# Re-ordering the prologue of a fused attention and GEGLU block: loads, statistics, transposes and weight re-ordering

## The chip, the cores and the metric

The kernel runs on one core of a Trainium2 chip. The metric is the time of one execution in microseconds (us) of device time. The engines named below are PE (TensorE, matmuls), DVE (VectorE), ACT (ScalarE), POOL (GpSimd) and SP (SyncE, which here only issues DMAs). Each engine executes its own list of instructions in order; they wait for each other with semaphores.

## The reference

One sequence of S = 2048 tokens of width D = 512, 32 heads of 16, and a GEGLU of width F = 1792, all bf16:

```python
def reference(A_x, A_wqkv, A_wo, B_x, B_w_gate, B_w_up, B_w_down):
    # _A_ref: q, k, v = split(x @ wqkv); p = softmax(q k^T / 4); (p v) @ wo
    # _B_ref: (gelu(x @ w_gate) * (x @ w_up)) @ w_down
    x = A_x
    h = x + _A_ref(_layernorm(x, axis=-1), A_wqkv, A_wo)
    h2 = h + _B_ref(_layernorm(h, axis=-1), B_w_gate, B_w_up, B_w_down)
    return h2
```

(`...` bodies are told in the comments; `_layernorm` has no weights, gelu is the tanh form.)

## The kernel before, in words

**How it is recorded.** `Plan` (line 16) records one instruction list per engine; `P.op` and `P.dma` add an instruction with the tiles that it reads and writes, and `Plan` derives the semaphore waits. So the order on each engine is the order in which the Python code calls `P.op`, fixed when the program is built.

**Tiles.** The 2048 tokens are 16 tiles `t` of 128, or 4 chunks `c` of 512. A *unit* is one *group* `gi` (256 queries, 8 groups) and one *slot* (4 heads, 8 slots): 64 units. For a unit, pass 1 computes the scores of all keys (line 772) and reduces their maximum on DVE (line 781, one reduce of 128x1024 a tick); POOL turns the maxima into a correction that is added to the queries (lines 792 to 826); pass 2, 24 ticks later, computes the scores again (line 842), ACT takes the exponential from PSUM to `PTM`, `PTE` or `PTG` (line 854), and PE multiplies by V (line 868, `item_pv`). A unit has 16 *ticks*; the main loop (line 1259) runs 1024 ticks of pass 1 and 24 more of pass 2 alone, 1048 in all. In the first 20 ticks (`DOUBLES`) the scores of two ticks are issued together.

**The dense stream.** All other PE work goes through `Dense` (line 482), a queue of items that the loop feeds piece by piece into the ticks: projections `item_projT` (K and Q, head tile `ht`, chunk `c`, line 645) and `item_projV` (line 709), transposes `item_xnT` (line 461), and after them, per group, `item_ofin`, `item_oproj`, and the FFN: seven pairs of `item_gate` and `item_up` (lines 1052 and 1066) and two `item_down` (line 1103). The list `qkv_items` (line 731) sets the order at the start. When its last item is done, `qkv_finished` (line 626) frees the SBUF of the projections and queues the FFN weights in twelve pieces, of which one is loaded in four of every 16 ticks (line 1312); the first group's FFN may start when all are issued (`add_ffn_when`, line 937). Items start under conditions that the builder estimates (bank free, ACT's lag `act_lag`, POOL's budget in `PoolStream`). A piece that does not fill its share of a tick is made up with dummy matmuls (line 1252).

**GELU by hand.** For groups 0 to 6 the gate tile is evicted to `g_sb`, three POOL operations (lines 1037 to 1039) prepare the argument, ACT takes the tanh (line 1030), two POOL operations (1035, 1036) and the product with `u_sb` (1089) write two chunks of `GUT`, which `item_down` reads. For the last group (7), ACT takes the GELU directly from PSUM (line 1060).

**The end.** `tail_b` (line 1196) closes the last unit's attention (`tail_norm`, `tail_onT`), the output projection, the second layer norm of group 7 (two POOL operations for the reciprocal root, lines 1217 and 1218; normalisation on DVE, line 1220), and in between feeds what is left in the dense stream (`fill`, line 1145). Then come the rest of the dense stream (line 1226), and the FFN of group 7 (line 1232).

**The prologue**, which the change touches. SP issues four loads of x (one a chunk), the Q and K weights as one load of 1024 KB, the V weights, and `wo`. Layer norm of a tile needs its statistics: by `stats_dve` (bn_stats and bn_aggr on DVE, line 355) or `stats_act` (two ACT passes with accumulation, line 359), then the reciprocal root on POOL (`rstd_bn`, `rstd_sums`, `rstd_pow`), then the normalisation (`norm1`, on DVE or POOL; `c3_act` on ACT). The normalised tile is transposed either by `xnT_pe` (four PE transposes, evicted by ACT, line 391) or by `xnT_dma` (a DMA transpose issued by SP, line 399; chunk 2 only). `w_order` (line 402) copies the Q or K weights of a head tile to the order in which the projection reads them. `warm` (line 413) issues dummy matmuls. The first two items, K and Q of the first head tile and chunk, are evicted directly to `KT` and `QT` (lines 661 and 659). `early` (line 754) says at which tick the rest of the prologue is issued: statistics and normalisation of chunk 3, and `w_order` for head tiles 1 to 3.

```python
        warm(16)
        for t in range(4):
            stats_dve(t)
        ...
        for t in range(4, 7):
            stats_act(t)
        stats_dve(7)
        stats_dve(8)
        ...
        for t in range(4):
            norm1(t, "dve")
            xnT_pe(t, 4 + t)
        warm(3)
        stats_dve(9)
        w_order("k", 0, "dve")
        w_order("q", 0, "dve")
```

## Time and profile before

| | |
|---|---|
| median of 3 runs | 1260.45 us (1260.25 to 1260.73) |
| the profiled execution | 1260.49 us, span 1258.8 us, mean granted PE clock 0.997 |
| busy of the span | PE 90%, DVE 95%, ACT 95%, POOL 60% |
| first reduce of line 781 starts | 16.97 us |
| thirteenth reduce starts | 36.48 us |
| last exponential of line 854 starts in the row at | 1225.38 us |
| weights for Q and K landed | 12.04 us after the span's start (issued 2.94, 9.1 to landing) |
| longest groups | DVE line 781, 1024 reduces, 1166.1 us; ACT line 854 to `PTM`, 1388 exponentials, 741.0 us |

All times within the profile are counted from the start of the span, of one profiled execution. A row of the timeline has its start, its duration, the engine, the line, the operation, `out<-in` with shapes, how many instructions are merged, and in brackets how long the engine idled before it and who ended the wait. "PEld" is the loading of weights into PE.

### The profile page before, as it was taken

The page shows a single profiled execution, that of the slowest core. Times are in us where ns is not written, and L with a number is a line of the kernel's source. Part 1 is how long each engine was busy: PE and PEld are TensorE (multiplying, and loading weights), DVE is VectorE, ACT ScalarE, POOL GpSimd, SP SyncE. Part 2 cuts the span into 40 slices and gives each one's busy share as a digit, 9 for nine tenths or more (in the row PEclk, how much of TensorE's full clock was granted, in tenths as well). Part 3 has the DMA queues.
Part 4 walks back from the last instruction along what each step waited for, and adds up shares of the span by engine and source line. Part 5 has one row for each costly group of instructions (what it writes and reads, how often), then busy time and mean ns, then how long its engine had stood idle before and what let it go on. Part 6 is the DMA issues. An engine that isn't in the chain of part 4 may idle for free.

```text
span 1258.8 us, 31261 instructions
## 1 busy us (share of the span) xinstructions
PE 1133.1 (90%) x12501; PEld 405.6 (32%) x12680; DVE 1194.0 (95%) x1090; ACT 1200.2 (95%) x2465; POOL 759.3 (60%) x1534
## 2 busy tenths in 40 slices
PE   6999888889999999989989998999999899899998
PEld 2322222233323333333323333233333333233335
DVE  8999999999999999999999999999999999999913
ACT  7799999999999999999999999999999999999992
POOL 7557775467746765386745766467653766457650
PEclk9999999999999999999999999999999999999999
DMA  5000004300010000100010000100001000100000
GB/s 166 27 26 27 24 18 123 93 5 4 6 30 12 6 5 6 38 5 6 4 26 18 6 4 6 30 12 6 7 5 37 5 6 4 26 19 6 4 12 17
DMA packets 51392, 27.98 MB, mean 22 GB/s; under 512 B 37168, under 2 KB 49712, under 8 KB 51248
## 3 DMA queue, kind: packets, MB, share of 16 engines
q1 hardware_dynamic: 51248, 25.97, 8.0%
q8 instruction: 101, 1.65, 0.6%
q14 instruction: 43, 0.35, 0.1%
HBM read 11.80 MB, written 2.10 MB: 11 GB/s over the span
## 4 chain that ended last, share of the span: by engine, by line
ACT 41%; DVE 27%; PE 26%; POOL 3%; issue 2%; DMA 1%; SPq 0%
DVE PM L781 27%; ACT PTM L854 23%; PE pbank L868 7%; ACT PTG L854 7%; PE pbank L842 4%; PE pbank L772 4%; ACT PTE L854 4%; PE pbank L1096 3%; PE pbank L1252 3%; ACT th_sb L1030 2%; ACT g_sb L613 1%; PE pbank L1047 1%; ACT OA L613 1%; DMA wqkv_sb<-in_A_wqkv_dram 1%; ACT OnT L987 1%
## 5 line engine op out<-in xcount | busy, mean ns | idle before, releaser
L781 DVE TENSOR_REDUCE PM<-pbank 128x2 f32<-128x1024 f32 x1024 | 1166.1, 1216 | 13.4 <-PE pbank L842 4.9
L854 ACT ACTIVATE PTM<-pbank 128x512 bf16<-128x512 f32 x1388 | 741.0, 671 | 13.5 <-PE pbank L842 6.4
L842 PE MATMUL pbank<-QT,KT 32*128 32x256 bf16 x4096 | 488.4, 273 | 5.2 <-ACT PTM L854 1.7
L772 PE MATMUL pbank<-KT,QT 32*128 32x512 bf16 x2048 | 394.1, 384 | 21.5 <-DVE PM L781 7.5
L1252 PE MATMUL pbank<-ones_bf,ident 128*128 128x512 bf16 x667 | 214.1, 383 | 49.3 <-ACT PTM L854 23.5
L854 ACT ACTIVATE PTG<-pbank 128x512 bf16<-128x512 f32 x420 | 228.8, 662 | 2.4 <-PE pbank L842 1.5
L772 PEld LDWEIGHTS pbank<-KT,QT 32*128 32x128 bf16 x2048 | 100.1, 91 | 354.3 <-DVE PM L781 166.1
L842 PEld LDWEIGHTS pbank<-QT,KT 32*128 32x128 bf16 x4096 | 159.6, 92 | 56.3 <-ACT PTM L854 28.4
L868 PE MATMUL pbank<-PTM,VA 128*17 128x256 bf16 x2776 | 154.9, 275 | 15.2 <-ACT PTM L854 0.6
L854 ACT ACTIVATE PTE<-pbank 128x512 bf16<-128x512 f32 x240 | 138.5, 671 | 2.0 <-PE pbank L842 0.7
L807 POOL TENSOR_TENSOR MX<-PM,MX 128x8 f32<-128x8 f32 x64 | 12.8, 200 | 163.2 <-DVE PM L781 163.2
L903 POOL TENSOR_TENSOR LINV<-OAT,negone 128x16 f32<-128x16 f32 (+1 forms) x32 | 92.6, 2895 | 4.3 <-DVE OAT L602 4.3
L1252 PEld LDWEIGHTS pbank<-ones_bf,ident 128*128 128x128 bf16 x821 | 50.0, 97 | 128.8 <-ACT PTM L854 81.9
L868 PEld LDWEIGHTS pbank<-PTM,VA 128*17 128x17 bf16 x2776 | 42.7, 87 | 107.5 <-PE pbank L868 73.9
L796 POOL TENSOR_TENSOR MX<-PM,MX 128x8 f32<-128x8 f32 x64 | 12.9, 201 | 100.2 <-DVE PM L781 99.8
L1047 PE MATMUL pbank<-hnT_l,wu_sb 128*128 128x256 bf16 x448 | 67.1, 275 | 3.5 <-ACT PTM L854 0.2
L1047 PE MATMUL pbank<-hnT_l,wg_sb 128*128 128x256 bf16 x448 | 67.1, 275 | 2.5
L1089 POOL TENSOR_TENSOR GUT<-th_sb,u_sb 128x512 bf16<-128x512 f32 x49 | 62.2, 1270 | 9.8 <-DVE u_sb L602 7.8
L1036 POOL TENSOR_TENSOR th_sb<-th_sb,g_sb 128x512 f32<-128x512 f32 x49 | 62.1, 1267 | 4.1
L1037 POOL TENSOR_TENSOR th_sb<-g_sb 128x512 f32<-128x512 f32 x49 | 50.9, 1039 | 22.0 <-ACT g_sb L613 22.0
L1039 POOL TENSOR_TENSOR th_sb<-th_sb,g_sb 128x512 f32<-128x512 f32 x49 | 62.0, 1265 | 3.1
L868 PE MATMUL pbank<-PTG,VA 128*17 128x256 bf16 x840 | 58.9, 275 | 3.5
(147 smaller groups left out, 1070.0 us busy)
## 6 DMA issues: line engine op xcount, KB each, us to landing
QKS<-QKS SPq DMA_DIRECT2D x27, 112.0 KB, 2.2
x_sb<-in_A_x_dram SPq DMA_DIRECT2D x4, 512.0 KB, 5.4
xres<-in_A_x_dram SPq DMA_DIRECT2D x16, 128.0 KB, 2.2
out_dram<-out_sb SPq DMA_DIRECT2D x16, 128.0 KB, 1.7
wg_sb<-in_B_w_gate_dram SPq DMA_DIRECT2D x4, 448.0 KB, 4.4
wu_sb<-in_B_w_up_dram SPq DMA_DIRECT2D x4, 448.0 KB, 4.1
wd_sb<-in_B_w_down_dram SPq DMA_DIRECT2D x3, 512.0 KB, 6.6
wqkv_sb<-in_A_wqkv_dram SPq DMA_DIRECT2D x1, 1024.0 KB, 9.1
```

Source lines behind the costliest of these rows:

```text
L772: P.op("pe", lambda e, g=g, b=b: e.matmul(pbank[:, b, :], QT[32 * g:32 * g + 32, c, slot, 128 * qt:128 * qt + 128], KT[32 * g:32 * g + 32, ...
L781: P.op("dve", lambda e: e.tensor_reduce(out=PM[:, par, qt, kc, g:g + 2], in_=pbank[:, b:b + 2, :], axis=AX.X, op=ALU.max), reads=[("pb", b ...
L842: P.op("pe", lambda e, kt=kt, i=i: e.matmul(pbank[:, b, 256 * i:256 * i + 256], KT[32 * g:32 * g + 32, slot, 128 * kt:128 * kt + 128], QT[ ...
L854: P.op("act", lambda e, b=b, pi=pi: e.activation(out=PTt(pi), in_=pbank[:, b, :], func=ACT.Exp), reads=[("pb", b)], writes=[("PT", pi)], e ...
L868: P.op("pe", lambda e, g=g, kt=kt, pi=pi, i=i: e.matmul(pbank[32 * g:32 * g + 17, b, 0:256], VA[:, kt, 4 * slot + g, :], PTt(pi)[:, 256 * ...
L903: P.op("pool", lambda e: e.tensor_tensor(out=li, in0=oat4[:, :, :, 16], in1=negone[:, 0:8 * ns].rearrange("p (q h) -> p q h", q=2), op=ALU ...
L1036: o(1.27, lambda e: e.tensor_tensor(out=ts_, in0=ts_, in1=gs, op=ALU.mult), [("th", par), ("g", par)])], then=done)
L1037: pool.add([o(1.04, lambda e: e.tensor_tensor(out=ts_, in0=gs, in1=gs, op=ALU.mult), [("g", par)], dE), o(0.62, lambda e: e.tensor_scalar( ...
L1039: o(1.27, lambda e: e.tensor_tensor(out=ts_, in0=ts_, in1=gs, op=ALU.mult), [("th", par), ("g", par)])], then=lambda: defer(TANH_LAG, lamb ...
L1047: P.op("pe", lambda e, dc=dc, fc=fc, i=i: e.matmul(pbank[:, b, 256 * i:256 * i + 256], w[:, dc, 128 * fc:128 * fc + 128], hT[:, dc, :], st ...
L1089: P.op("pool", lambda e: e.tensor_tensor(out=o_ap, in0=shp(ts_), in1=shp(us), op=ALU.mult), reads=[("th", par), ("u", par)], writes=o_keys ...
L1252: P.op("pe", lambda e: e.matmul(pbank[:, b, :], ident[:], ones_bf[:, 0:512], start=True, stop=True), reads=["ident", "ones_bf"], writes=[( ...
```

## The change

- **Loads.** x chunks 0 and 1, then the Q and the K weights of head tile 0 alone (two loads of 128 columns, 256 bytes a row and 128 KB each), then x chunks 2 and 3, the V weights, the other Q and K weights (two loads of 384 columns), `wo`.
- **Statistics.** DVE: tiles 0 to 2, 6, 7, 9 to 13; ACT: 3 to 5, 8, 14, 15 (before: DVE 0 to 3, 7 to 10, 12, 13, 15; ACT 4 to 6, 11, 14). Tiles 10 and 11 of chunk 2 are now taken just before and in tick 0, and chunk 2's POOL work (`c2_rest`) is issued there too. Tiles 6 and 7 are normalised on POOL instead of DVE.
- **Transposes.** Chunk 2 is transposed on PE and evicted by ACT like the others (items `tr[8]` to `tr[11]`); the DMA transposes are gone. Of the first four tiles, DVE evicts the last.
- **Weight re-ordering.** Head tile 0: Q on DVE, K on ACT, ahead of the first normalisations; head tiles 1 to 3, on ACT, at ticks 9, 11, 16, 18, 20, 22 instead of 2, 5, 7, 9, 11, 13.
- **Order of the dense items.** Fewer V projections early (four instead of five before the last K of head tile 0, three in a row later); for head tiles 1 to 3 the first Q goes ahead of the four K.
- **Warming.** 26 dummy matmuls instead of 16, and 4 instead of 3 behind the first transposes.

```diff
-        for c in range(NCH):
-            P.dma("sp", lambda e, c=c: e.dma_start(out=x_sb[:, 4 * c:4 * c + 4, :], in_=xv[:, 4 * c:4 * c + 4, :]),
-                  ("x", c), writes=[("x", c)])
-        P.dma("sp", lambda e: e.dma_start(out=wqkv_sb[:, :, 0:2 * D], in_=wv[:, :, 0:2 * D]), "wqk", writes=["wqk"])
+        def load_qk(h0, h1, key):
+            for w_ in range(2):
+                P.dma("sp", lambda e, w_=w_: e.dma_start(out=wqkv_sb[:, :, D * w_ + 128 * h0:D * w_ + 128 * h1], in_=wv[:, :, D * w_ + 128 * h0:D * w_ + 128 * h1]), (key, w_), writes=[(key, w_)])
...
+        load_x(0)
+        load_x(1)
+        load_qk(0, 1, "wqka")
+        load_x(2)
+        load_x(3)
         P.dma("sp", lambda e: e.dma_start(out=wqkv_sb[:, :, 2 * D:3 * D], in_=wv[:, :, 2 * D:3 * D]), "wqkv", writes=["wqkv"])
+        load_qk(1, 4, "wqkb")
...
-        warm(16)
-        for t in range(4):
+        warm(26)
+        for t in range(3):
             stats_dve(t)
-        rstd_bn(0, 4)
+        for t in (3, 4, 5):
+            stats_act(t)
+        rstd_sums(3, 4)
+        rstd_bn(0, 3)
         rstd_pow(0, 4)
...
+        stats_dve(6)
         stats_dve(7)
+        w_order("q", 0, "dve")
+        w_order("k", 0, "act")
+        rstd_sums(4, 6)
+        rstd_bn(6, 8)
         rstd_pow(4, 8)
+        nmr(6, 8)
+        for t in (6, 7):
+            norm1(t, "pool")
         for t in range(4):
             norm1(t, "dve")
-            xnT_pe(t, 4 + t)
-        warm(3)
+        for t in range(4):
+            xnT_pe(t, 4 + t, "act" if t < 3 else "dve")
+        warm(4)
+        stats_act(8)
         stats_dve(9)
...
+        for t in (4, 5):
             norm1(t, "dve")
+
+        def c2_rest():
+            rstd_sums(8, 9)
+            rstd_bn(9, 12)
+            rstd_pow(8, 12)
+            nmr(8, 12)
+            for t in range(8, 12):
+                norm1(t, "pool")
...
-        kq = [it for ht in range(1, 4) for it in [(item_projT, "k", ht, c) for c in range(NCH)] + [(item_projT, "q", ht, 0)]]
+        kq = [it for ht in range(1, 4) for it in [(item_projT, "q", ht, 0)] + [(item_projT, "k", ht, c) for c in range(NCH)]]
...
-        qkv_items = [(item_projT, "k", 0, 0), (item_projT, "q", 0, 0), tr[4], tr[5], tr[6], tr[7], k0[0], vs[0], vs[1], vs[2], vs[3], vs[4], k0[1], tr[12], tr[13], tr[14], tr[15], k0[2]]
-        vs = vs[5:]
-        for it in kq[:5]:
-            qkv_items += [it, vs.pop(0)]
+        qkv_items = [(item_projT, "k", 0, 0), (item_projT, "q", 0, 0), tr[4], tr[5], tr[6], tr[7], k0[0], vs[0], vs[1], tr[8], tr[9], tr[10], tr[11], k0[1], vs[2],
+                     tr[12], tr[13], tr[14], tr[15], k0[2], vs[3]]
+        vs = vs[4:]
+        for it, n_ in zip(kq[:5], (1, 1, 1, 3, 1)):
+            qkv_items += [it] + vs[:n_]
+            vs = vs[n_:]
         qkv_items += vs + kq[5:]
...
-        for t in range(8, 12):
-            xnT_dma(t)
+        stats_dve(10)
...
-        early = {0: [lambda: stats_act(14), lambda: stats_dve(12)], 1: [lambda: stats_dve(13)], 2: [lambda: stats_dve(15), c3_rest, lambda: w_order("k", 1, "act")],
-                 7: [c3_act, lambda: w_order("k", 2, "act")],
-                 5: [lambda: w_order("q", 1, "act")], 9: [lambda: w_order("q", 2, "act")],
-                 11: [lambda: w_order("k", 3, "act")], 13: [lambda: w_order("q", 3, "act")]}
+        early = {0: [lambda: stats_dve(11), c2_rest, lambda: stats_act(14)], 1: [lambda: stats_dve(12), lambda: stats_act(15)], 2: [lambda: stats_dve(13), c3_rest],
+                 7: [c3_act], 9: [lambda: w_order("q", 1, "act")], 11: [lambda: w_order("k", 1, "act")], 16: [lambda: w_order("q", 2, "act")],
+                 18: [lambda: w_order("k", 2, "act")], 20: [lambda: w_order("q", 3, "act")], 22: [lambda: w_order("k", 3, "act")]}
```

More of the change, by code (lines that the diff above doesn't have):

```diff
@@ L329, in bass_sequential_preLN__mha_block__geglu_ffn__prompt_kernel, with load_x @@
         g_h = lambda gi, k: xres[:, 2 * (gi % 2) + k, :]
-        for c in range(NCH):
-            P.dma("sp", lambda e, c=c: e.dma_start(out=x_sb[:, 4 * c:4 * c + 4, :], in_=xv[:, 4 * c:4 * c + 4, :]),
-                  ("x", c), writes=[("x", c)])
-        P.dma("sp", lambda e: e.dma_start(out=wqkv_sb[:, :, 0:2 * D], in_=wv[:, :, 0:2 * D]), "wqk", writes=["wqk"])
+        def load_x(c):
+            P.dma("sp", lambda e: e.dma_start(out=x_sb[:, 4 * c:4 * c + 4, :], in_=xv[:, 4 * c:4 * c + 4, :]), ("x", c), writes=[("x", c)])
+        def load_qk(h0, h1, key):
[6 more added lines that the diff above has]
+        load_x(3)
         P.dma("sp", lambda e: e.dma_start(out=wqkv_sb[:, :, 2 * D:3 * D], in_=wv[:, :, 2 * D:3 * D]), "wqkv", writes=["wqkv"])
+        load_qk(1, 4, "wqkb")
         P.dma("sp", lambda e: e.dma_start(out=wo_sb[:], in_=A_wo.rearrange("(c p) j -> p c j", p=128)), "wo", writes=["wo"])
@@ L389, in norm1, with xnT_pe @@
                  reads=[("x", t // 4), ("rstd", t), ("mv", t)], writes=[("xn", t)])
-        def xnT_pe(t, b):
+        def xnT_pe(t, b, eng="act"):
             pt = pbank[:, b, :].bitcast(BF16)
@@ L395, in xnT_pe @@
                      reads=[("xn", t), "ident"], writes=[("pb", b)], sig=(dc == 3))
-            P.op("act", lambda e: e.activation(out=xnT[:, :, 128 * t:128 * t + 128], in_=pt[:, 0:512].rearrange("p (c s) -> p c s", c=4), func=ACT.Copy),
-                 reads=[("pb", b)], writes=[("xnT", t)])
-        def xnT_dma(t):
-            P.dma("sp", lambda e: e.dma_start_transpose(out=xnT[:, :, 128 * t:128 * t + 128], in_=xn_sb[:, t, :]), ("xnT", t), reads=[("xn", t)], writes=[("xnT", t)])
+            o_ap, i_ap = xnT[:, :, 128 * t:128 * t + 128], pt[:, 0:512].rearrange("p (c s) -> p c s", c=4)
+            if eng == "act":
+                P.op("act", lambda e: e.activation(out=o_ap, in_=i_ap, func=ACT.Copy), reads=[("pb", b)], writes=[("xnT", t)])
+            else:
+                P.op("dve", lambda e: e.tensor_copy(out=o_ap, in_=i_ap), reads=[("pb", b)], writes=[("xnT", t)])
         def w_order(which, ht, eng):
@@ L405, in w_order @@
             i_ap = wqkv_sb[:, :, base + 128 * ht:base + 128 * ht + 128].rearrange("p c (s g i) -> p c s g i", s=2, g=4)
+            rd = [("wqka" if ht == 0 else "wqkb", 0 if which == "q" else 1)]
             for s_ in range(2):
@@ L408, in w_order @@
                 if eng == "act":
-                    P.op("act", lambda e, oo=oo, ii=ii: e.activation(out=oo, in_=ii, func=ACT.Copy), reads=["wqk"], writes=[(nm, ht, s_)])
+                    P.op("act", lambda e, oo=oo, ii=ii: e.activation(out=oo, in_=ii, func=ACT.Copy), reads=rd, writes=[(nm, ht, s_)])
                 else:
-                    P.op(eng, lambda e, oo=oo, ii=ii: e.tensor_copy(out=oo, in_=ii), reads=["wqk"], writes=[(nm, ht, s_)])
+                    P.op(eng, lambda e, oo=oo, ii=ii: e.tensor_copy(out=oo, in_=ii), reads=rd, writes=[(nm, ht, s_)])
         def warm(n):
@@ L415, in warm @@
                 P.op("pe", lambda e: e.matmul(pbank[:, 0, :], ident[:], ones_bf[:, 0:512], start=True, stop=True), reads=["ident", "ones_bf"], writes=[("pb", 0)], sig=False)
-        warm(16)
-        for t in range(4):
+        warm(26)
+        for t in range(3):
             stats_dve(t)
-        rstd_bn(0, 4)
+        for t in (3, 4, 5):
+            stats_act(t)
+        rstd_sums(3, 4)
+        rstd_bn(0, 3)
         rstd_pow(0, 4)
-        for t in range(4, 7):
-            stats_act(t)
+        stats_dve(6)
         stats_dve(7)
-        stats_dve(8)
-        rstd_sums(4, 7)
-        rstd_bn(7, 8)
+        w_order("q", 0, "dve")
+        w_order("k", 0, "act")
+        rstd_sums(4, 6)
+        rstd_bn(6, 8)
         rstd_pow(4, 8)
+        nmr(6, 8)
+        for t in (6, 7):
+            norm1(t, "pool")
         for t in range(4):
             norm1(t, "dve")
-            xnT_pe(t, 4 + t)
-        warm(3)
+        for t in range(4):
+            xnT_pe(t, 4 + t, "act" if t < 3 else "dve")
+        warm(4)
+        stats_act(8)
         stats_dve(9)
-        w_order("k", 0, "dve")
-        w_order("q", 0, "dve")
-        stats_act(11)
-        stats_dve(10)
-        rstd_bn(8, 11)
-        rstd_sums(11, 12)
-        rstd_pow(8, 12)
-        nmr(8, 12)
-        for t in range(8, 12):
-            norm1(t, "pool")
-        for t in range(4, 8):
-            norm1(t, "dve")
+        for t in (4, 5):
+            norm1(t, "dve")
+        def c2_rest():
[5 more added lines that the diff above has]
+                norm1(t, "pool")
         def c3_rest():
             rstd_bn(12, 14)
-            rstd_sums(14, 15)
-            rstd_bn(15, 16)
+            rstd_sums(14, 16)
             rstd_pow(12, 16)
@@ L627, in qkv_finished @@
             qkv_over[0] = True
-            fk = [("xnT", t) for t in range(NT)] + ["wqkv", "wqk"] + [(nm_, h_, s_) for nm_ in ("wq_r", "wk_r") for h_ in range(4) for s_ in range(2)] + [("QKS", i_) for i_ in range(4)] + [("QKS2", i_) for i_ in range(2)]
+            fk = [("xnT", t) for t in range(NT)] + ["wqkv"] + [(k_, w_) for k_ in ("wqka", "wqkb") for w_ in range(2)] + [(nm_, h_, s_) for nm_ in ("wq_r", "wk_r") for h_ in range(4) for s_ in range(2)] + [("QKS", i_) for i_ in range(4)] + [("QKS2", i_) for i_ in range(2)]
             dF = rdeps("F", fk)
@@ L746, in bass_sequential_preLN__mha_block__geglu_ffn__prompt_kernel @@
         p1_begun[0] = True
-        for t in range(8, 12):
-            xnT_dma(t)
+        stats_dve(10)
         dense.banks, dense.rr = [6, 7], 0
```

## The prediction

> **What bounds the kernel now.** I read the chain of work that ended last first, then the costliest groups, then the start and the end of the timeline, because the diff touches the start only and the order listing (below) shows that the end changes too. The page:

> ```profile
> ACT 41%; DVE 27%; PE 26%; POOL 3%; issue 2%; DMA 1%; SPq 0%
> ...
> L781 DVE TENSOR_REDUCE PM<-pbank 128x2 f32<-128x1024 f32 x1024 | 1166.1, 1216 | 13.4 <-PE pbank L842 4.9
> ```

> The reader is to see one row of 1024 reduces that keeps DVE busy for 1166 us with 13.4 us of idle before it: from the first reduce to the last, the body is paced by DVE, handing over to ACT where ACT has more to do. So the start can give back only (a) the time before the first reduce and (b) the holes between the first reduces. The timeline of the start (start, duration, engine, line) shows (a):

> ```profile
> 12.07 0.36 DVE L411 COPY wk_r<-wqkv_sb 128x256 bf16<-128x256 bf16 x2 [0.28 <-DMA wqkv_sb<-in_A_wqkv_dram]
> ...
> 12.70 1.87 PE L648 MATMUL pbank<-xnT,wk_r 128*128 128x512 bf16 x4 [0.38 <-DVE wq_r L411]
> ...
> 16.97 1.23 DVE L781 TENSOR_REDUCE PM<-pbank 128x2 f32<-128x1024 f32 x1 [1.46 <-PE pbank L772]
> ```

> The first projection starts as the weights (landed 12.04) are re-ordered; the first reduce follows at 16.97. DVE's timeline shows (b); eight reduces stand ahead of these rows, and from 36.48 on they run on:

> ```profile
> 28.73 2.36 DVE L781 TENSOR_REDUCE PM<-pbank 128x2 f32<-128x1024 f32 x2 [0.19 <-PE pbank L772]
> 32.73 2.36 DVE L781 TENSOR_REDUCE PM<-pbank 128x2 f32<-128x1024 f32 x2 [1.64 <-PE pbank L772]
> 36.48 4.62 DVE L781 TENSOR_REDUCE PM<-pbank 128x2 f32<-128x1024 f32 x4 [1.40 <-PE pbank L772]
> ```

> The clock, in the table by stretches (PE's busy time first, the granted clock behind POOL), falls to half after PE stood idle:

> ```profile
> 12.00:14.00 2.00, 1.62 (x5) 0.51 (x5) 1.90 (x8) 1.88 (x6) 0.91 (x2) 0.50 1.06 335
> ...
> 32.00:36.00 4.00, 3.37 (x15) 1.13 (x12) 2.36 (x2) 2.63 (x6) 0.00 (x0) 0.57 0.00 0
> ```

> The end: PE alone carries the last group's FFN, in the chain from 1236.88 (its first gate matmul starts at 1236.72 in the timeline). What follows that matmul takes 1258.8 - 1236.72 = 22.1 us in either kernel. In the timeline of the end:

> ```profile
> 1229.03 0.69 DVE L602 COPY u_sb<-pbank 128x512 f32<-128x512 f32 x1
> ...
> 1236.72 1.04 PE L1047 MATMUL pbank<-hnT_l,wg_sb 128*128 128x256 bf16 x8
> ```

> Only one `up` tile (1229.03) and the down projection of the group before are left between the last exponential and those gates. POOL's timeline gives the price of one GELU by hand:

> ```profile
> 1206.43 1.04 POOL L1037 TENSOR_TENSOR th_sb<-g_sb 128x512 f32<-128x512 f32 x1
> 1207.56 0.62 POOL L1038 TENSOR_SCALAR th_sb<-th_sb 128x512 f32<-128x512 f32 x1
> 1208.26 1.27 POOL L1039 TENSOR_TENSOR th_sb<-th_sb,g_sb 128x512 f32<-128x512 f32 x1
> ...
> 1212.41 0.62 POOL L1035 TENSOR_SCALAR th_sb<-th_sb 128x512 f32<-128x512 f32 x1 [0.95 <-ACT th_sb L1030]
> 1213.11 1.27 POOL L1036 TENSOR_TENSOR th_sb<-th_sb,g_sb 128x512 f32<-128x512 f32 x1
> 1214.34 1.27 POOL L1089 TENSOR_TENSOR GUT<-th_sb,u_sb 128x512 bf16<-128x512 f32 x1
> ```

> Three POOL operations 3.10; the tanh on ACT, 0.80 (0.08 after POOL, and L1035 starts 0.72 after the tanh's 1211.69); two more 1.93; GUT 1.30: 7.13 us for one pair of gate and up tiles when nothing overlaps.

> **Step 1, the way to the first reduce.** x chunks 0 and 1 still land at 4.8 and 6.3. The 256 KB of weights for the first heads come next, 1024 packets of 256 B. In the trace's packet records 256 B took 18 ns on one of 16 engines, 1 KB 46 ns; 64 packets each give 1.2 to 2.9 us, landed at 7.5 to 9.2. DVE gets to re-ordering q at 8.9 (five pairs of statistics at 0.80 from 4.81), ACT to k at 9.0 (three tiles of sums at 1.38, 1.4 us ahead of today): cost 0 to 0.2, taken as 0. Reciprocal roots for tiles 0 to 3 come 1.36 after their last statistic, 8.7 (now 9.55), so norms run from 9.2 (now 9.61). Transposes follow 0.45 behind; three evictions on ACT at 0.50, the fourth on DVE at 0.42 (row of L1189): ready at 11.6; four warming matmuls end at 11.8. The projection starts then, not at 12.70, and at full clock, since 26 instead of 16 warming matmuls (10 x 0.213 more) leave PE idle 0.7 us, not 3.2. K and Q take 0.85 each instead of about 1.6. QT is evicted at 13.75 (now 15.79), the first reduce starts at 14.9: **2.1 us earlier**.

> **Step 2, the holes.** All transposes on PE: chunk 2 loses four DMA transposes (5.2 us of SP, which nobody on the path waits for) and gains 16 transposes and four ACT evictions, 4 x 0.55 = 2.2 us. ACT then runs without a gap from QT: four evictions and two QKE copies to 17.2, sums 18.6, KT of chunk 1 19.3, copy 19.8, sums 21.2, two V 22.1, four evictions 24.5. K of chunk 2 on PE then, 0.85 at full clock or 1.7 at half; V behind it, ahead of the scores of ticks 8 and 9. Reduce 9 starts at 26.8 or 28.5 (now 28.73). PE has only 1.7 us of work in the 4.1 before, so half clock is near. Chunk 3 ends its POOL norms at 26.7 (now 26.6), so it follows ACT: its four evictions come 2.0 or 0.4 earlier, and so does reduce 13. I take the middle: **1.2 us gained in all by reduce 13**, bounds 0.3 and 5.4 (no hole: 14.9 + 5.85 for three reduces with statistics + 9 x 1.14 = 31.1 against 36.48).

> **Step 3, moved work, at nothing.** Re-ordering of the other heads (12 x 0.41) moves to ticks 9 to 22; ACT idles about 0.7 a tick between 36 and 50 us, which hides it; without that cover it would cost 2. Two more V evictions come after tick 24: 2 x 0.06, nothing.

> **Step 4, the end.** This comes from the listing of both built programs, engine by engine, in which ticks can be counted by the score matmuls. The last QKV item ends at tick 161 (before 147), the first FFN gate at 223 (203), and group 1's at 351 (320). The delay never heals: in every later group the gates come 31 ticks late, and when the 1048 ticks end, group 6 has 4 of 7 gates and ups done, against 7 and 6. So the tail holds three gates and three ups instead of one up. Their GELUs stand on POOL in the fixed order 3+2 operations of pair 4, the last group's two rstd operations, GUT 4, all of pair 5, all of pair 6; on ACT pair 4's tanh stands ahead of the copies of h. The matmuls of down stand on PE behind that, and the last group's gates behind down. On the clock of before:

> - gate 4 is evicted at 1229.03, where up stands now; POOL starts 0.77 later, 1229.80 (as GUT does now); 3.10 + 0.80 + 1.93 gives 1235.63;
> - h, 0.63 behind the tanh, gives statistics at 1235.0, no wait; rstd to hn 1.14 (1232.25 to 1233.39), 1236.77; up 4 behind hn on DVE at 1237.43; GUT 4 from 1238.20 to 1239.50;
> - pairs 5 and 6: 2 x 7.13, 1253.76;
> - PE: two matmuls and the residual of the first down, 15 of the second: 18 x 0.216 (12 in 2.59 in the chain) = 3.9: 1257.7 against 1236.72: **21.0 us later**.

> PE idles 6.7 us ahead of these 18. In both rows above PE stays at half for 2.3 to 2.4 us after it restarts, 5.6 matmuls at 0.427 instead of 0.216: 1.2. **Tail 22.2**.
> [...]

> **Step 5, the body.** Five evictions (0.49) and three tanhs (0.52) leave ACT's body, 4.0 us, the upper bound of a gain. Where no FFN runs the chain has 116 reduces in 131.31 us, 1.132; with FFN 350 in 400, 1.143; 20 ticks less of that are 0.2, which I take. Shifted by 31 ticks, FFN evictions meet exponentials at other ticks: up to 2 either way.

> **Sum:** the profiled execution took 1260.49 (span 1258.8), the median of the runs is 1260.45: 1260.5 - 1.2 - 0.2 + 22.2 = 1281.3, so 1281.

> **Rivals.**
> - *The start pays in full.* DVE never waits after 14.9: 5.4 instead of 1.2, 1277. For it: the work of chunks 2 and 3 fits by bytes; against: ACT's line of step 2. Chance 0.20.
> - *The tail hides, and it gets faster.* GELUs run under the last group's normalisation; only the matmuls of five items show, 5 x 0.87 = 4.4, with 5.4 from the start and 4.0 from ACT: 1255.5. It decides from where the last GUT is written before about 1237 on the old clock. Against: POOL's order and 7.13 us a pair. Chance 0.05, a fifth of it within 0.2%.
> - *PE stays slow.* All 18 matmuls at 0.427 (3.8 instead of 1.2), the start gains nothing, and the body loses 2: 1287. [...] Chance 0.10.
> - *It does not do what it says:* the small packets land late, past 9.2, and DVE, in order, holds the norms. No gain, 1282.5; chance 0.03, beside the forecast.

> The forecast itself (1276 to 1286) has 0.62. The range goes over the first rival's bound and the clock's: 1275 to 1286. About 0.2% (2.5 us) is what a measurement here can tell from no change: faster 0.04, same 0.01, slower 0.95, the first two from the second rival alone.

> **What would show it.** First reduce near 14.9; the thirteenth between 31 and 36; the table of clocks at 1.00 from 11 to 16 us; in the tail, POOL busy without a break of 1 us for some 24 us, PE idle behind it, the first of the last group's gates 22 us before the end, and the last reduce within 3 us of today's. If PE reaches the last gates within 5 us of their old distance from the last exponential, step 4 is wrong, and with it the sign.

## The result, and the profile after

The changed kernel takes **1281.8 us** (median of 4 runs, 1280.29 to 1282.19) against 1260.35 (4 runs, 1260.14 to 1260.73) beside it: ratio 1.0168, 95% interval 1.0152 to 1.0184, slower by 21.5 us. The profiled execution took 1282.19 us, span 1280.3.

The chain of the work that ended last and two of the costliest groups, of the changed kernel (lines below the prologue are 15 higher than before):

```profile
ACT 38%; DVE 30%; PE 25%; POOL 4%; issue 2%; DMA 0%; POOLq 0%; DVEq 0%
...
L796 DVE TENSOR_REDUCE PM<-pbank 128x2 f32<-128x1024 f32 x1024 | 1166.5, 1216 | 11.9 <-PE pbank L857 5.3
...
L1111 PE MATMUL pbank<-wd_sb,GUT 128*128 128x512 bf16 x209 | 61.1, 404 | 13.8 <-POOL GUT L1104 9.3
```

The 1024 reduces are as long as before and wait 1.5 us less. The loss is not there: the third row shows PE waiting 9.3 us for POOL's GUT (the product of gate and up) ahead of the down projection, a wait that its group before (L1096) does not have.

The start, in DVE's timeline:

```profile
14.85 1.22 DVE L796 TENSOR_REDUCE PM<-pbank 128x2 f32<-128x1024 f32 x1 [0.37 <-PE pbank L787]
...
31.16 2.36 DVE L796 TENSOR_REDUCE PM<-pbank 128x2 f32<-128x1024 f32 x2 [1.32 <-PE pbank L787]
35.47 10.27 DVE L796 TENSOR_REDUCE PM<-pbank 128x2 f32<-128x1024 f32 x9 [1.95 <-PE pbank L787]
```

The first reduce is 2.1 us earlier (16.97), the thirteenth only 1.0 (36.48). The table of stretches shows the clock at half in two places between them; PEclk is the third figure from the end:

```profile
20.00:22.00 2.00, 2.00 (x6) 0.60 (x4) 1.97 (x4) 1.62 (x5) 2.00 (x3) 0.61 0.19 57
...
32.00:34.00 2.00, 2.00 (x6) 0.69 (x5) 1.52 (x2) 0.84 (x3) 0.30 (x2) 0.50 0.03 8
```

The end, in the timelines of POOL and of PE:

```profile
1235.94 1.27 POOL L1104 TENSOR_TENSOR GUT<-th_sb,u_sb 128x512 bf16<-128x512 f32 x1 [1.52 <-DVE u_sb L617]
...
1243.12 1.26 POOL L1104 TENSOR_TENSOR GUT<-th_sb,u_sb 128x512 bf16<-128x512 f32 x1
...
1250.29 1.26 POOL L1104 TENSOR_TENSOR GUT<-th_sb,u_sb 128x512 bf16<-128x512 f32 x1
```

```profile
1251.61 1.03 PE L1111 MATMUL pbank<-wd_sb,GUT 128*128 128x512 bf16 x2 [6.14 <-POOL GUT L1104]
1252.44 0.63 PE L1115 MATMUL pbank<-xres,ident 128*128 128x512 bf16 x1
1252.87 5.33 PE L1111 MATMUL pbank<-wd_sb,GUT 128*128 128x512 bf16 x14
1258.04 0.38 PE L1115 MATMUL pbank<-xres,ident 128*128 128x512 bf16 x1
1258.25 1.04 PE L1062 MATMUL pbank<-hnT_l,wg_sb 128*128 128x256 bf16 x8
```

Three GUT tiles, 7.18 and 7.17 us apart; PE idles 3.20 us for the second and 6.14 for the third. The last group's gates start at 1258.25 (before: 1236.72) and the span ends 22.05 us later, as before (22.1). From the first FFN piece behind the last exponentials to those gates it is 33.28 us (1224.97 to 1258.25), before 9.43 (1227.29 to 1236.72): the end costs 23.85, and start and body together give back 2.32 (1227.29 - 1224.97).

### The profile page after: what moved, and what is told of

Same layout as the page of the kernel before. It is cut to its first block, busy times and chain, and to the rows that moved or that the text cites. A ratio compares the mean times of both kernels' runs of the same rounds, so it can differ in the third digit from the quotient of the medians.

```text
span 1280.3 us, 31344 instructions
## 1 busy us (share of the span) xinstructions
PE 1142.7 (89%) x12532; PEld 409.0 (32%) x12719; DVE 1196.1 (93%) x1090; ACT 1202.8 (94%) x2469; POOL 765.5 (60%) x1541
## 3 DMA queue, kind: packets, MB, share of 16 engines
q8 instruction: 101, 1.65, 0.5%
## 4 chain that ended last, share of the span: by engine, by line
ACT 38%; DVE 30%; PE 25%; POOL 4%; issue 2%; DMA 0%; POOLq 0%; DVEq 0%
DVE PM L796 29%; ACT PTM L869 21%; ACT PTG L869 7%; PE pbank L883 7%; PE pbank L787 5%; PE pbank L857 4%; PE pbank L1111 4%; ACT PTE L869 4%; PE pbank L1267 3%; ACT th_sb L1045 2%; ACT g_sb L628 1%; PE pbank L1062 1%; ACT u_sb L628 1%; ACT OnT L1002 1%; ACT xres L995 1%
## 5 line engine op out<-in xcount | busy, mean ns | idle before, releaser
L796 DVE TENSOR_REDUCE PM<-pbank 128x2 f32<-128x1024 f32 x1024 | 1166.5, 1216 | 11.9 <-PE pbank L857 5.3
L787 PE MATMUL pbank<-KT,QT 32*128 32x512 bf16 x2048 | 394.2, 384 | 21.2 <-DVE PM L796 6.9
L1267 PE MATMUL pbank<-ones_bf,ident 128*128 128x512 bf16 x678 | 217.5, 383 | 46.6 <-ACT PTM L869 21.6
L883 PE MATMUL pbank<-PTM,VA 128*17 128x256 bf16 x2776 | 154.9, 275 | 14.8 <-ACT PTM L869 0.6
L1111 PE MATMUL pbank<-wd_sb,GUT 128*128 128x512 bf16 x209 | 61.1, 404 | 13.8 <-POOL GUT L1104 9.3
```

What stands on the lines that cost most here:

```text
L787: P.op("pe", lambda e, g=g, b=b: e.matmul(pbank[:, b, :], QT[32 * g:32 * g + 32, c, slot, 128 * qt:128 * qt + 128], KT[32 * g:32 * g + 32, ...
L796: P.op("dve", lambda e: e.tensor_reduce(out=PM[:, par, qt, kc, g:g + 2], in_=pbank[:, b:b + 2, :], axis=AX.X, op=ALU.max), reads=[("pb", b ...
L883: P.op("pe", lambda e, g=g, kt=kt, pi=pi, i=i: e.matmul(pbank[32 * g:32 * g + 17, b, 0:256], VA[:, kt, 4 * slot + g, :], PTt(pi)[:, 256 * ...
L1111: P.op("pe", lambda e: e.matmul(pbank[:, b, :], GUT[:, fc, 128 * k:128 * k + 128], wd_sb[:, fc, :], start=(fc == 0), stop=False), reads=[( ...
L1267: P.op("pe", lambda e: e.matmul(pbank[:, b, :], ident[:], ones_bf[:, 0:512], start=True, stop=True), reads=["ident", "ones_bf"], writes=[( ...
```

## The experiments

Twelve kernels, in the order of their runs. "The slip" is the delay of step 4: the last QKV item ends 14 ticks later, and from the second group (group 1) on the FFN runs 31 ticks later. Ratios are to the kernel before, beside them on the same chip.

**The slip removed (e1).** FFN weights may be loaded at six ticks of sixteen.

```diff
-            if w_pieces and tick % 16 in (7, 9, 11, 13):
+            if w_pieces and tick % 16 in (3, 5, 7, 9, 11, 13):
```

> The changed kernel, with one edit: pieces of FFN weights may be loaded at six ticks of every sixteen (3, 5, 7, 9, 11, 13) and not at four (7, 9, 11, 13). In the built order the first FFN gate then stands at tick 204 and not at 223, group 1 at 320 and not at 351, and the tail keeps no gate and one up, as the kernel before has it. The prologue is that of the changed kernel. Theory (the whole loss is the 31 ticks by which the FFN slips into the tail; the prologue itself gains): the last group's gates start about 11 us behind the last exponential's work again, the tail costs nothing, and the time is 1260.4 less the start's gain of 1.0 and up to 1.3 more: 1258 to 1259.5. Rival (the loss has another cause in the change, such as transposes on TensorE or later re-ordering): the time stays at 1275 to 1282.

Measured: 1259.74 us, ratio 0.9989 (0.9981 to 0.9998). One line of the builder's timing takes the whole 21.5 us away, with the new prologue in place: the slip is the loss. In PE's records the last QKV item still ends at tick 161, but the first gate stands at 204 and not at 223, and group 1's at 320 and not at 351. The tail waits for a single GUT, at 1229.41, and the gates start at 1236.33:

```profile
1236.12 0.38 PE L1115 MATMUL pbank<-xres,ident 128*128 128x512 bf16 x1
1236.33 1.04 PE L1062 MATMUL pbank<-hnT_l,wg_sb 128*128 128x256 bf16 x8
```

**The slip alone (e2).** The kernel before, with only the order of that list changed.

```diff
-  ... for it in [(item_projT, "k", ht, c) for c in range(NCH)] + [(item_projT, "q", ht, 0)]]
+  ... for it in [(item_projT, "q", ht, 0)] + [(item_projT, "k", ht, c) for c in range(NCH)]]
```

> The kernel before, with one edit: for head tiles 1 to 3 the q projection stands ahead of the four k projections in the list of QKV items, as the change has it. Nothing else of the prologue changes. In the built order the last QKV item then ends at tick 161 and not 147, the first gate stands at tick 223, group 1 at 351 and three gates and three ups are left to the tail. Theory (the order of this one list makes the slip, and the slip is the loss): first reduce at 16.97 and thirteenth at 36.5 as in the kernel before, the tail longer by 23.9, the body shorter by about 1.3: 1281.5 to 1284, so slower than the changed kernel by about 1.0. Rival (the slip or the loss needs the other edits of the prologue): 1259 to 1262.

Measured: 1283.8 us, ratio 1.0181 (1.0167 to 1.0195). First reduce 16.95, thirteenth 36.46, as before; in PE's timeline the tail of the changed kernel:

```profile
1252.92 1.03 PE L1096 MATMUL pbank<-wd_sb,GUT 128*128 128x512 bf16 x2 [6.57 <-POOL GUT L1089]
...
1259.07 1.04 PE L1047 MATMUL pbank<-hnT_l,wg_sb 128*128 128x256 bf16 x8
```

So one reordered list, whose own instructions cost nothing where they stand, costs 23 us some 1200 us later.

**POOL's chain taken out of the tail (e3).** The leftover gates go through ACT's GELU and the product on DVE (same function).

```diff
-            if gi == GL:
+            if gi == GL or in_tail[0]:
```

(in `item_gate` and in `item_up`; `tail_b` sets the flag.)

> The changed kernel, with one edit: the three gates left to the tail go through ACT's GELU and DVE's product, as the last group's do, in place of the five operations on POOL with ACT's tanh (the same function). The slip of 31 ticks stays. Theory (the tail's price is POOL's serial chain of 7.13 us a pair, and what PE loses behind it): only the matmuls of five more items, 5 x 0.87 = 4.4, and waits of 0 to 2 remain of the 23.9: 1262 to 1265. Rival A (the left-over matmuls and their order on PE cost the time, whoever computes the GELU): over 1275. Rival B (in the tail all of it hides, as in the second rival of the prediction): 1258 to 1260.

Measured: 1263.19 us, ratio 1.0021 (1.0011 to 1.0030). PE's timeline:

```profile
1230.42 1.05 PE L1062 MATMUL pbank<-hnT_l,wu_sb 128*128 128x256 bf16 x8 [1.13 <-DVE GUT L1092]
...
1231.76 3.19 PE L1112 MATMUL pbank<-wd_sb,GUT 128*128 128x512 bf16 x13
...
1238.23 1.04 PE L1062 MATMUL pbank<-hnT_l,wg_sb 128*128 128x256 bf16 x8
```

From the first FFN piece of the tail (1223.28) to the last group's gates it is 14.95, 5.5 more than before: the matmuls of five items (5 x 0.87 = 4.4) and the wait of 1.13 for DVE's product. Of the 23.85, 5.5 is this, and 18.3 is POOL's chain with what PE loses behind it.

**PE kept busy in the tail (e4).** Its dummy matmuls write a free bank that nobody reads.

```diff
+                if in_tail[0] and k == 0 and fc in (10, 12):
+                    dummy(banks.free[0], 16 if fc == 10 else 26)
```

> The changed kernel, with one edit: 16 and 26 matmuls whose result nobody reads, into a free bank, ahead of the down projection's chunks 10 and 12 in the tail, where PE stands idle for 6 us each waiting for the last two GUT tiles. POOL's chain stays. Theory (the 18 matmuls behind the last GUT took 6.64 and not 3.9 since PE restarts at half clock): they take 3.9 to 4.2, and the time falls by 2.4 to 2.7, to 1279.0 to 1279.5. Rival (the 6.64 are waits for banks or for the residual's copies, not the clock): no change, 1281 to 1282.5, or slower if the matmuls reach past the GUT.

Measured: 1278.7 us, ratio 1.0145 (1.0131 to 1.0158), by the ratios 2.9 us under the changed kernel. The 18 matmuls take 3.90 (1251.10 to 1255.00) in place of 6.64:

```profile
1244.18 5.78 PE L1271 MATMUL pbank<-ones_bf,ident 128*128 128x512 bf16 x26
1251.10 0.38 PE L1111 MATMUL pbank<-wd_sb,GUT 128*128 128x512 bf16 x1 [1.15 <-POOL GUT L1104]
...
1255.00 1.04 PE L1062 MATMUL pbank<-hnT_l,wg_sb 128*128 128x256 bf16 x8
```

PE's clock is 1.00 there (3.90 / 18 = 0.217 a matmul), so the 2.74 us that differ were the clock, not waits.

The next four start from e1, so without the slip, and ask what the prologue itself gives.

**Short warming (e5).** `warm(26)` and `warm(4)` back to `warm(16)` and `warm(3)`.

> The changed kernel with the six load slots (so without the slip into the tail), and with the warming matmuls of the kernel before: 16 and 3 in place of 26 and 4. Theory (part of the earlier first reduce is the clock, as step 1 had it: K and Q of chunk 0 take 0.85 each at full and 1.6 at half clock): PE idles about 3 us before the projection again, K and Q take 1.4 to 1.6 each, the first reduce comes at 15.8 to 16.6 and not at 14.8 to 15.1. The total follows only as far as the holes behind the eighth reduce do not swallow it: 1259.7 to 1260.8. Rival (the projection starts when xnT is ready, and the clock there is full anyway): first reduce within 0.3 of 15.1.

Measured: 1258.88 us, ratio 0.9985 (0.9976 to 0.9994). In this profile both expectations missed: the first reduce came at 14.61, earlier than either said, with the clock at 1.00 from 10 to 14 and PE idle 1.59 ahead of the transposes. These start at 9.43; in e1 they stand behind the 26 warming matmuls and start at 9.94. In e10 below, with the same short warming, the theory held (table by stretches):

```profile
10.00:14.00 4.00, 4.00 (x25) 2.49 (x24) 2.95 (x8) 2.99 (x8) 3.48 (x8) 0.62 1.10 336
```

There PE idled 2.23, the clock was 0.62, and the first reduce came at 16.00. So the short warming is a draw, not a fixed cost. Over all profiles, the clock was full from 10 to 16 us in each of the eight with 26 warming matmuls; of the six with 16 it was full in two (e5 and e12) and fell to half between 9.6 and 11.7 in four.

**Weights behind x (e6).**

```diff
-        load_x(0); load_x(1); load_qk(0, 1, "wqka"); load_x(2); load_x(3); ... wqkv ...; load_qk(1, 4, "wqkb")
+        for c in range(NCH): load_x(c)
+        load_qk(0, 1, "wqka"); load_qk(1, 4, "wqkb"); ... wqkv ...
```

> The changed kernel with the six load slots, and with the loads issued in another order: x chunks 0 to 3 first, then the weights of the first heads, then the other heads', then v's. Theory (the earlier first reduce comes from the weights landing ahead of chunks 2 and 3): the weights land 2 to 3.5 us later, DVE's re-ordering stands in front of the norms and the first projection waits for it; first reduce at 16.5 to 18, that is most of the 2.1 lost; total 1260 to 1262. Rival (the earlier norms and the longer warming do it, and the weights were early enough either way): first reduce within 0.4 of 15.1, total within 0.5 of 1259.7.

Measured: 1261.47 us, ratio 1.0004 (0.9995 to 1.0013). DVE's timeline:

```profile
9.84 0.36 DVE L419 COPY wq_r<-wqkv_sb 128x256 bf16<-128x256 bf16 x2 [1.07 <-DMA wqkv_sb<-in_A_wqkv_dram]
...
15.76 1.23 DVE L794 TENSOR_REDUCE PM<-pbank 128x2 f32<-128x1024 f32 x1
```

The first reduce is between the two expectations, the time in the theory's range. Even behind all of x, the 128 KB for Q have landed at 9.82 and those for K at 10.36, where the 1024 KB of the kernel before landed at 12.04. Yet the first projection starts at 12.65, as before (12.70): the 1.2 us by which the first reduce is ahead (15.76, before 16.97) go with the clock, which is full here and was at half from 11.7 to 15.1 there. The place in the queue is worth 0.6 to 0.9 us more (15.11 in e1, 14.85 in the changed kernel).

**Chunk 2 by DMA transposes (e7).** `tr[8]` to `tr[11]` leave the list, which has the old order in the first ticks; four `dma_start_transpose` come back.

> The changed kernel with the six load slots, and with chunk 2 transposed by four DMAs again and the items of the first ticks in the order of the kernel before. Theory (step 2: four transposes' evictions, 4 x 0.55 = 2.2 us of ACT, stand in front of chunk 2's projection, and PE and ACT pay for them): the hole ahead of the ninth reduce stays or moves to where the DMA transposes land, ACT's evictions for chunk 3 come about 2 us earlier, and the thirteenth reduce comes at 33 to 35 in place of 35.4: 1257.5 to 1259.5. Rival (chunk 3 hangs on POOL's norms, which end near 26.7, and on the half clock behind them, not on ACT): thirteenth reduce at 35 to 37, total 1259.5 to 1261.

Measured: 1260.65 us, ratio 0.9996 (0.9987 to 1.0005). The hole moved ahead of the ninth reduce:

```profile
28.54 2.36 DVE L798 TENSOR_REDUCE PM<-pbank 128x2 f32<-128x1024 f32 x2 [2.30 <-PE pbank L789]
```

The thirteenth comes at 34.47, 19.80 behind the first with the clock at 1.00 throughout; transposes on PE take 18.4 at full clock (below). So transposes on PE, with the new order of items, are the better choice up to the thirteenth reduce, by 1.4, where the clock holds. The thirteenth reduce is the theory's and the total the rival's: no more than 1 us can be told here.

**Much filling (e8).** Dummies behind the transposes of six tiles, into the score bank that is written next.

```diff
+        FILL = {6: 3, 7: 4, 12: 3, 13: 4, 14: 2, 15: 4}
...
             xnT_pe(t, b)
+            if t in FILL and p1_begun[0]:
+                dummy(2 * (p1_ring[0] % 3), FILL[t])
```

> The changed kernel with the six load slots, and with two to four matmuls whose result nobody reads behind the transposes of tiles 6, 7 and 12 to 15, into the score bank that the next scores overwrite, so that PE does not stand idle there. Theory (the holes ahead of reduces 11 and 13 are half clock: K of chunk 3 takes 1.7 and V 1.9 in place of 0.85 and 0.95): K and V of chunk 3 at 0.85 to 1.0 each, the thirteenth reduce at 33 to 34 in place of 35.4, total 1258 to 1258.8. Rival (the dummies themselves stand in front of the transposes and projections, and what is gained at the clock is lost in the queue): thirteenth reduce at 35 or later, total 1259.5 to 1261.

Measured: 1259.94 us, ratio 0.9994 (0.9985 to 1.0003). The clock is 1.00 throughout, and the time is no better: the rival. In PE's timeline the last four dummies stand ahead of the scores that DVE waits 2.96 us for:

```profile
31.37 1.04 PE L1271 MATMUL pbank<-ones_bf,ident 128*128 128x512 bf16 x4
32.34 0.39 PE L791 MATMUL pbank<-KT,QT 32*128 32x512 bf16 x4
```

**The slots alone (e9).** e1's line in the kernel before.

> The kernel before, with the six load slots alone. The first gate then stands at tick 191 in place of 203; groups 1 to 6 and the tail stand as before. Theory (the slots gain nothing by themselves; what the changed kernel with six slots gains, 1.4 us by the ratio, is its prologue): first reduce at 16.97, thirteenth at 36.5, total within 0.6 of the kernel before. Rival (the slots are the gain, the new prologue none): 1.0 to 1.6 below the kernel before.

Measured: 1259.81 us, ratio 0.9991 (0.9982 to 1.0000): 1.1 under the kernel before, as e1 (0.9989). That is the rival's range (1.0 to 1.6), though the interval reaches into the theory's; the gain of e1 can't be credited to the prologue.

**Little filling (e10), and with the long warming (e11).** e8's edit with `FILL = {12: 2, 13: 2}`, on e5 and on e1.

> The changed kernel with the six load slots and with the warming matmuls of the kernel before (16 and 3), and with two matmuls whose result nobody reads behind the transposes of tiles 12 and 13 only, where PE waits for the norms of chunk 3, and none ahead of the scores. Theory (of the 3.7 us between the ninth and the thirteenth reduce that are not reduces, about 2 are half clock; the larger filling gave them back since its last matmuls stood ahead of the scores in PE's queue): clock 1.00 from 28 to 36, thirteenth reduce at 32.8 to 33.8 in place of 35.0, total 1257 to 1258.2. Rival (even small dummies cost as much as the clock gives, or the order of transposes ahead of scores sets the time): thirteenth at 34.5 or later, total 1258.5 to 1260.

> The kernel of e10 with the long warming of the changed kernel (26 and 4) in place of 16 and 3. In the profile of e10 the clock was at half from 10 to 14 us and the first reduce came at 16.00; in that of e5, with the same short warming, it was full and the first reduce came at 14.61. Theory (the short warming leaves a gap of 1.6 us and with it a half clock in some executions; the long one closes the gap; from the first to the thirteenth reduce the new prologue takes 18.4 at full clock): clock 1.00 from 10 to 36, first reduce at 14.8 to 15.1, thirteenth at 33.2 to 33.6, total 1256.8 to 1258.0, so a ratio to the kernel before of 0.997 to 0.998. Rival (what the first reduce gains is lost again in the holes, as in the other runs): thirteenth at 34.4 or later, total 1258 to 1259.5.

Measured: e10 1258.1 us, ratio **0.9977 (0.9967 to 0.9987)**, the lowest ratio of this study, though its interval overlaps those of e5, e11 and e12; e11 1258.76, 0.9981 (0.9972 to 0.9990). In e10, DVE's timeline and the clock where both lost it before:

```profile
31.67 2.36 DVE L800 TENSOR_REDUCE PM<-pbank 128x2 f32<-128x1024 f32 x2 [1.32 <-PE pbank L791]
34.41 11.46 DVE L800 TENSOR_REDUCE PM<-pbank 128x2 f32<-128x1024 f32 x10 [0.38 <-PE pbank L791]
```

```profile
32.00:34.00 2.00, 1.92 (x12) 0.72 (x12) 2.00 (x2) 1.48 (x5) 0.62 (x1) 1.00 0.02 8
```

The hole ahead of the thirteenth reduce is 0.38 in place of 1.95. The 1.32 ahead of the eleventh stays at full clock: there the scores stand behind chunk 3's transposes on PE. In e11 the early half (18 to 22 us) lost its clock all the same; the thirteenth reduce at 34.55 and the median are the rival's figures, the ratio is just outside the theory's. Its first reduce was late already, at 15.39, and there the long warming itself stood in the way: the clock was at half until 7.58, the 26 matmuls took 8.66 us from 1.73, and the transposes behind them started at 10.23, 1.06 behind the first norm (0.46 in e5). In e10 it was the first reduce that came late (16.00, see e5), so its thirteenth missed the expected 33.8 although nothing was lost between: 18.41.

**The old prologue with slots and filling (e12).**

> The kernel before with the six load slots and with the small filling of e10 (two matmuls whose result nobody reads behind the transposes of tiles 12 and 13), so e11 with the old prologue. Theory (the new prologue is worth about 1 us by itself, once the clock holds): the filling takes the half clock out of 32 to 36 here too, thirteenth reduce at 34.8 to 35.4 in place of 36.1 to 36.5, ratio to the kernel before 0.9986 to 0.9993, so 0.6 to 1.3 us slower than e10 and e11. Rival (the gain of e10 and e11 is slots and filling alone, the new prologue gives nothing): ratio 0.9976 to 0.9983, as e10 and e11.

Measured: 1258.76 us, ratio 0.9984 (0.9975 to 0.9993), between theory and rival, thirteenth reduce at 35.10. Against e10 and e11 the old prologue loses 0.4 to 0.9 us, less than the intervals can tell. What the new prologue is worth by itself is thus between nothing and 1 us, and stays open.

## Why the prediction was right

**The forecast, 1281.3, held within 0.5 us of the median;** the sign, the mechanism and its place are those of step 4. Two terms of the sum were mis-sized, by 1.65 and 1.1 us in opposite directions: that the number came so near is luck, the sign and the mechanism are not.

- *Step 1* (2.1 earlier): 2.1, in the two parts that the step had, an earlier projection (11.74, before 12.70) and full clock for K and Q. The reason given for the clock, the longer warming, holds only in part: e5 shows full clock without it, e10 and its 0.62 the case that it guards against. The old prologue at full clock (e12) has its first reduce at 16.06, the new one at half (e10) at 16.00: each part alone gives about 1 us.
- *Step 2* (1.2 by the thirteenth reduce): 1.0 in the profile of the changed kernel. Its bounds were set by ACT's chain and by K of chunk 2, "0.85 at full clock or 1.7 at half". That K (25.37) ran at full clock; the half clock fell on two V projections before it (18.95, eight matmuls in 3.18 us; in e3 four take 1.04) and on K and V of chunk 3 (1.68 and 1.91). So the middle came out near by another way than the step's, which is luck. The cost isn't fixed either. The changed kernel, e3 and e4 issue the same instructions up to the tail, and from first to thirteenth reduce they took 20.62, 18.42 and 19.70. A stretch of 2 us was at half for (1 - clock) x 2 x 2 us; summed from 16 to 38 that is 6.8, 0 and 3.4 us. So each spell lasts 3.4 us and costs 0.9 to 1.3; e1 (6.8 us at half, 20.27) and e10 (none, 18.41) fit. The clock records of the kernel before have its two spells from 11.69 and from 32.17, those of the changed kernel from 18.16 and from 31.82, each 3.41 us long.
- *Step 3* (nothing): right. From the start of reduce 13 to that of reduce 200, over the moved re-ordering, it is 213.3 us before and after.
- *Step 4, the chain* (21.0): right. The last GUT ended 26.58 us behind the tail's first FFN matmul (1251.55 - 1224.97); the sum had 1253.76 - 1227.29 = 26.47. The sign that POOL would be busy without a break of 1 us missed by one wait, 1.52 us for `u_sb` ahead of the first GUT (shown above).
- *Step 4, "half clock 1.2"*: **mis-sized**. The 18 matmuls took 6.64, not 3.9 + 1.2: half clock cost 2.74 (e4), and 2.25 in e2 (1252.92 to 1259.07). The two rows that gave 2.4 us at half held only the part of a spell that came behind the restart. The table by stretches, around the restart at 1251.61:

```profile
1251.00:1255.00 4.00, 3.39 (x9) 1.20 (x9) 0.69 (x1) 0.00 (x0) 0.55 (x1) 0.50 0.10 30
1255.00:1259.00 4.00, 4.00 (x18) 1.97 (x17) 0.55 (x1) 0.00 (x0) 0.00 (x0) 0.72 0.02 7
```

  Half until about 1257.2 (0.28 x 2 x 4 us into the second row), 5.6 us behind the restart and not 2.4; in the clock records the spell is 13.7 us long and began at 1243.55. The range of the forecast also goes over a bound for the clock ("the clock's") that no run shows; what the runs showed in its place is the cost above, 2.74 and 2.25 against 1.2, and 23.85 for the end against 22.2.
- *Step 5* (0.2 gained): **mis-sized**, 1.3 (the tail's first FFN matmul is 2.32 earlier, and 1.02 of that come from the start). From reduce 200 to 300 it is 114.91 before and 114.03 after, from 300 to 500 230.01 and 229.51; e2 has the same 114.03 and 229.51, so the slip alone does it. DVE's idle time ahead of reduces from 249 to 364 us is 1.1 before and 0.6 after. The reverse eats e1's start: ahead by 1.1 at reduce 13 and at 200, it is ahead by 0.4 at 300 (115.59 for those hundred, e9 114.27). DVE's groups from 249 to 364 us, e1 and then e9, idle time in the last columns:

```profile
L796 DVE TENSOR_REDUCE PM<-pbank 128x2 f32<-128x1024 f32 x100 | 114.1, 1216 | 1.6 <-PE pbank L857 1.3
```

```profile
L781 DVE TENSOR_REDUCE PM<-pbank 128x2 f32<-128x1024 f32 x102 | 115.9, 1215 | 0.7 <-PE pbank L842 0.5
```

  0.9 of the 1.3 is DVE waiting for PE's scores as the FFN sets in; why more in e1, and the other 0.4, was not traced.
- *The rivals.* "The start pays in full" asked for no hole after 14.9; no run of the new prologue came under 18.4 from first to thirteenth reduce. "The tail hides" fell in e2 and the changed kernel, and e3 shows what it would have needed: without POOL's chain, 5.5 stay. "PE stays slow" had its 18 matmuls at half throughout; 13 of 18 were (2.74 / 0.211). "It does not do what it says" fell: the Q and K weights of head tile 0 landed at 7.11 and 7.65, and DVE copied Q at 8.97 without a wait.

The slip itself was read from the listing of the built programs and not explained. e2 shows which edit makes it, e1 what turns it into a loss. The last QKV item ends at tick 161 in place of 147; the twelve pieces of FFN weights are queued only then, and each must meet one of four ticks of sixteen. Counted in PE's records, the first gates of groups 1, 2 and 3 stand at ticks 320, 448 and 576 before and at 351, 479 and 607 after: 128 apart in both, so the 31 ticks are never made up. Why the reordered list ends 14 ticks later, and why a group that is behind is not worked off faster, stays open.

## What to carry to other kernels

Before reordering the start of a kernel whose later work is fed into the ticks of a loop, compare the built order at the *end*: here 14 ticks in one list became 31, and three GELUs by hand with nothing to hide behind. Price what falls out of the loop by the slowest engine's serial chain, not by its matmuls: 7.2 us a pair against 4.4 for five items. And a first instruction that comes 2 us earlier is worth no more than what the next holes leave; follow the count of reduces until both kernels run at the same pace.

## What the runs showed of the hardware

```profile
27.48:30.90 3.42, 1.63 (x19) 0.88 (x20) 2.63 (x3) 3.34 (x7) 3.24 (x6) 1.00 0.11 34
```

```profile
28.06:31.48 3.42, 2.67 (x28) 1.25 (x24) 2.36 (x2) 3.34 (x7) 3.24 (x7) 1.00 0.11 34
```

- In e1 the clock fell at 30.90, in e11 it held. e11's stretch from 14.41 to 17.82, which no dummy reaches, had 1.38 us, and the clock fell at 17.82. e3 kept 1.00 without any dummies: where the stretches begin differs from run to run (the first full clock at 4.86 us in the kernel before, 4.51 in the changed kernel, 7.58 in e11), and the emptiest of e3 had 1.83. So a clock of 1.00 in one profile does not tell filling from luck, but the matmul time of the stretches does.
- Dummies had a price where something that is waited for stood behind them: e8's twenty held the clock, the last four of them ahead of scores that DVE waited 2.96 us for, and nothing that could be measured was gained over e1 (ratio 0.9994, e1 0.9989).
